# Storing the last group in chunks, counting the conditions earlier, and loading one input group in halves

## The chip, the cores and the metric

The kernel runs on one core of a Trainium2 chip. The metric is device time in microseconds (us). The engines are TensorE (PE, with PEld for its weight loads), VectorE (DVE), ScalarE (ACT), GpSimd (POOL) and SyncE (SP); SP and POOL issue the transfers here.

## What is computed

Attention with 32 inducing points, then a hardswish feed-forward block, for x of 4 x 12480 x 128:

```python
def _attn_ref(x, inducing):
    B, N, C = x.shape
    scale = 1.0 / np.sqrt(C)
    I = np.broadcast_to(inducing[None], (B, m, C))
    def mab(q, kv):
        s = scale * (q @ kv.transpose(0, 2, 1))
        s = s - s.max(-1, keepdims=True)
        a = np.exp(s)
        a /= a.sum(-1, keepdims=True) + 1e-09
        return a @ kv
    h = mab(I, x)
    return mab(x, h)

def _moe_ref(x, w_in, w_out):          # 128 -> 2048 -> 128
    h = x @ w_in
    return (h * np.clip(h + 3.0, 0.0, 6.0) / 6.0) @ w_out
```

## The kernel before

**Tiling.** Each of the 4 batches of 12480 tokens is cut into six full groups of 2048 tokens (128 partitions x 16, 1 MB of float32) and a rest of 192 (48 x 4). A group is cut into chunks of 4 tokens per partition (512 tokens), so a batch has 25 chunks and the program 100. Group g is full for 0 to 5; group 6 is the rest.

**Two phases per batch.** The first (names with `a_`, and `a_first` for batch 0) casts x to bf16 (`xb`), transposes it on PE (`pt`, copied to `xT`), forms the weights of the 32 points (`s`, then `Exp` to `a`) and sums `hnd`. From this the coefficients follow (`c_` functions, `c_first` for batch 0): the transposed summary `HT` by way of `htp` and the reciprocal `rD`, its bf16 differences `dH`, the products `gp` and `dpm`, the squares `sq`, and at the end `Cq` and `BD`. The second phase (`b_`) makes the output chunk by chunk: `b_pack` and `b_spread` give the factor tile `d` (SP copies one quarter of `dk` over the partitions, 128 KB), `b_base` gives `TF` through `bp` on PE and Exp on ACT, `b_prod` multiplies `TF` by `d` on DVE to `TD`, `b_lin` and `b_quad` accumulate `op` on PE, `b_r` gives the factor `r_all`, and `b_evac` multiplies `op` by it into `os` on DVE.

**Order.** The schedule is written out by hand: the main loop (line 873) goes through the 100 chunks, and in batch b's chunks the work of batch b + 1 is interleaved by shares. In iteration t it first evacuates chunk t - 1, then works on PE for chunk t; `TD` is made one iteration ahead. The two `op` buffers in PSUM mean that chunk t needs the evacuation of chunk t - 2. The last batch has nothing to interleave. For batch 0, `a_first` works in half groups: per piece, cast (partly on ACT, partly on DVE), transposes of the next piece, weights, sum of the piece before.

**Queues.** POOL issues all loads of x and of the weights, and the stores of batches 0 to 2; SP issues the spreads of `d` and the stores of the last batch. On each the order of the program is kept. A full group of output is one store of 1 MB after its fourth chunk (line 842).

**The end.** The second phase rests on conditions on the data (bounds on the factors, the denominators and the hidden values). After the last chunk five counts on DVE (lines 924 to 939) look over all of them, PE sums the counts over the partitions (`cp5`, line 941), DVE compares the sum with the expected number (`bad_i`), and only then `b_evac` of the last chunk follows (line 946). All engines load `bad_i` (line 949) and branch on it (line 952): a direct path is there for data that don't meet the conditions. The path isn't taken here.

**Dummy products.** `warm(n)` issues n products on a zero tile, so that PE stays busy; `c_first` has them at lines 629, 633 and 635.

Of the kernel before, what the change touches and what calls it, by code (L numbers as in the profile page):

```python
# [9 lines left out]
FP32 = mybir.dt.float32  # L10
# [4 lines left out]
ALU = mybir.AluOpType  # L15
AX = mybir.AxisListType
# [8 lines left out]
TG = 16  # L25
SL = 4
XBUF = 5
# [13 lines left out]
def kernel(  # L41
# [8 lines left out]
    nc = tc.nc  # L50
    P = nc.NUM_PARTITIONS
    B, N, C = x.shape
    M = inducing.shape[0]
# [15 lines left out]
    NGR = len(groups)  # L69
# [4 lines left out]
    NCK = len(chunks)  # L74
    first_chunk = [chunks.index((g, 0)) for g in range(NGR)]

    keep = ctx.enter_context(tc.tile_pool(name="keep", bufs=1))
# [3 lines left out]
    with ExitStack() as es:  # L81
# [14 lines left out]
        cst = es.enter_context(tc.tile_pool(name="cst", bufs=1))  # L96
# [10 lines left out]

        xs, xbs = {}, {}

        def load_x(b, g, parts=1):  # L110
            t0, p, n = groups[g]
            src = x[b, t0 : t0 + p * n, :].rearrange("(p i) c -> p i c", i=n)
            if n < TG:
                t = xlast.tile([P, n, C], FP32R, name="xl")
            elif b == 0 and g == XBUF:

                t = osp.tile([P, TG, C], FP32R, name="x5", tag="os")
            else:
                t = xin.tile([P, TG, C], FP32R, name="xr")
            for h in range(parts):  # L120
                lo, hi = h * n // parts, (h + 1) * n // parts
                nc.gpsimd.dma_start(t[:p, lo:hi, :], src[:, lo:hi, :])
            xs[(b, g)] = t

        load_x(0, 0, 2)

        held = []
        NF = NGR - 1 if rest else NGR
# [34 lines left out]

        make_identity(nc, ident[:, :])
        for g in (NF, *range(1, XBUF + 1)):
            load_x(0, g, 2 if g in (XBUF - 1, XBUF) else 1)
        wake = const.tile([P, 512], BF16, name="wake")
        nc.vector.memset(wake[:, :], 0.0)
        ident_b = const.tile([P, P], BF16, name="ident_b")
# [2 lines left out]
        def warm(n):  # L172

            wp = psF.tile([P, 512], FP32, name="wp", tag="fb")
            for _ in range(n):
                nc.tensor.matmul(wp[:, :], lhsT=wake[:, :P], rhs=wake[:, :])
# [34 lines left out]
        NR = B * NCK * SL  # L211
# [415 lines left out]
        def c_first():  # L627

            warm(2)
            nc.scalar.copy(w_in_b[:, : F // 2], w_in_r[:, : F // 2].bitcast(FP32))  # L630
            c_den(0)
            nc.scalar.copy(w_in_b[:, F // 2 :], w_in_r[:, F // 2 :].bitcast(FP32))
            warm(2)
            c_HT(0)
            warm(1)

            def cast_w(i, j):
                nc.scalar.copy(w_out_b[:, i:j, :], w_out_r[:, i:j, :].bitcast(FP32))

            cast_w(0, 4)  # L640
            c_G(0, 0, 6)
            sq = lambda *jbs: [c_sq(0, jb) for jb in jbs]
            cs = lambda *jcs: [c_C(0, jc) for jc in jcs]

            sg = lambda jb: (c_sq(0, jb), c_G(0, jb + 6, jb + 7))
            sg(0)
            sg(1)
            sg(2)
            cast_w(4, 8)
            b_pack(0, 0)  # L650
            b_e(0, 0)
            for c in range(4):
                b_spread(0, c)
            load_held(3)
            for jb in range(3, 7):
                sg(jb)
                cs(jb - 3)
            cast_w(8, 12)
            sg(7)
            b_f(0, 0)  # L660
            cs(4)
            sg(8)
            b_base(0, 0, 0)
            cs(5)
            sg(9)
            c_hs(0)
            b_base(0, 0, 1)
            cs(6)
            cast_w(12, 16)
            sq(10)  # L670
            cs(7)
            sq(11)
            b_r(0, 0)
            cs(8)
            sq(12)
            cs(9)
            sq(13)
            cs(10)
            b_base(0, 1, 0)
            sq(14)  # L680
            cs(11)
            sq(15)
            cs(12)
            c_L(0, 0)
            c_L(0, 1)
            b_base(0, 1, 1)
            a_cast(1, 0, ((nc.scalar.copy, 0, 2), (nc.scalar.copy, 2, 4)))
            b_prod(0, 0)
            c_BD(0)
            cs(13, 14, 15)  # L690
            c_tail(0)
            b_pack(0, 1)
            b_e(0, 1)
            c_max(0)
# [131 lines left out]
        def b_evac(b, c, op):  # L826
            g, j = chunks[c]
            t0, p, n = groups[g]
            st = S[b]
            if j == 0:  # L830
                st["os"] = osp.tile([P, TG, C], FP32, name="os", tag="os")
            ot = st["os"]
            nc.vector.tensor_mul(  # L833
                ot[:p, j * SL : (j + 1) * SL, :],
                op[:p, :].rearrange("p (s c) -> p s c", c=C),
                r_all[:p, b, c, :].unsqueeze(2).to_broadcast([p, SL, C]),
            )
            if (j + 1) * SL == n:
                r0 = b * N + t0

                eng = nc.gpsimd if b < B - 1 else nc.sync
                eng.dma_start(  # L842
                    out[r0 : r0 + p * n, :].rearrange("(p i) c -> p i c", i=n), ot[:p, :n, :]
                )


        a_begin(0)
        a_first()
        c_first()
        queue = []  # L850
        total = B * NCK
        ahead, sums = {}, {}
        for b in range(B):
            for g in range(NGR):
# [18 lines left out]
        for t in range(total):  # L873
# [10 lines left out]
            def bg(part):  # L884
                fill(n_units * (t - begin + part) / span)

            if t == total - NCK // 2:

                nc.gpsimd.drain()
# [29 lines left out]
            b_quad(bo, co, 3, op)  # L919
            evac = (bo, co, op)  # L920

        cnt = cst.tile([P, 5], FP32, name="cnt")
        junk = cst.tile([P, NR], FP32, name="junk", tag="r6")
        nc.vector.tensor_scalar(
            junk[:, :NR], r_all[:, :, :, :].rearrange("p b c s -> p (b c s)"), 1.0e-16, None,
            op0=ALU.is_ge, op1=ALU.add, accum_out=cnt[:, 0:1],
        )
        nc.vector.tensor_scalar(
            junk[:, : B * NGR], nf_all[:, :], -1.0e-8, None, op0=ALU.is_le, op1=ALU.add, accum_out=cnt[:, 1:2]
        )  # L930
        nc.vector.tensor_scalar(
            junk[:, :B], g_all[:, :], 3.0, None, op0=ALU.is_le, op1=ALU.add, accum_out=cnt[:, 2:3]
        )
        nc.vector.tensor_scalar(
            junk[:, : B * M], d_all[:, :, :].rearrange("p b m -> p (b m)"), 1.0e-20, None, op0=ALU.is_ge, op1=ALU.add, accum_out=cnt[:, 3:4]
        )
        nc.vector.tensor_scalar(
            junk[:, : B * M], d_all[:, :, :].rearrange("p b m -> p (b m)"), 1.0e30, None, op0=ALU.is_le, op1=ALU.add, accum_out=cnt[:, 4:5]
        )
        cp5 = psF.tile([P, 512], FP32, name="cp5", tag="fb")  # L940
        nc.tensor.matmul(cp5[:1, :5], lhsT=ones[:, 0:1], rhs=cnt[:, :])
        cs = cst.tile([1, 1], FP32, name="cs")
        nc.vector.tensor_reduce(cs[:, :], cp5[:1, :5], axis=AX.X, op=ALU.add)
        good = float(P * (NR + B * NGR + B + 2 * B * M))
        nc.vector.tensor_scalar(bad_i[:, :], cs[:, :], good, None, op0=ALU.not_equal)
        b_evac(*evac)


    bad = nc.values_load(
# [150 lines left out]
```

## Time and profile before

| | us |
|---|---|
| median of 4 runs (312.69 to 313.84) | 313.65 |
| the profiled execution, whole | 313.53 |
| its span, first to last instruction | 311.7 |
| PE busy | 299.2 |
| DVE busy | 236.5 |
| ACT busy | 231.6 |
| granted PE clock, mean | 0.993 |
| last matmul of the last chunk ends | 304.9 |
| store of the last full group issued / of the rest issued | 304.5 / 307.3 |

All times of the profile are us from the start of the span. A row of the timeline gives start, length, engine, line, operation, output<-input and shape, and in brackets the idle time before it and what ended it. A row of a tile's or line's view gives durations in ns (smallest, median, largest) and the first and last start. Instructions that only issue transfers, wait or branch are not counted as busy; they stand under the engine's queue (SPq for SP's).

### The profile page before, as it was taken

How to read it: one execution, taken by the hardware profiler on the slowest of the kernel's cores; microseconds unless marked ns; L12 is line 12 of the kernel's file. 1: busy time of each engine (PE TensorE's matmuls, PEld its weight loads, DVE VectorE, ACT ScalarE, POOL GpSimd, SP SyncE). 2: the span in 40 equal slices, each digit the busy share in tenths (PEclk: the TensorE clock that was granted, in tenths of full speed). 3: DMA queues.
4: the chain of work that ended last, by engine and by line, in shares of the span. 5: the costliest groups of instructions: out<-in, count | busy, mean ns of one | idle time of the engine just before them, and what ended most of it. 6: DMA issues, size and time to landing. Idle time of an engine off the chain costs nothing.

```text
span 311.7 us, 9605 instructions
## 1 busy us (share of the span) xinstructions
PE 299.2 (96%) x3930; PEld 233.5 (75%) x3930; DVE 236.5 (76%) x539; ACT 231.6 (74%) x425; POOL 34.6 (11%) x81
## 2 busy tenths in 40 slices
PE   8799999999999999999999999999999999999991
PEld 3697678887676878888767877888867786777781
DVE  1797796978883868878796668787788477888883
ACT  3788999886589678886679859888658945777750
POOL 7511301111100010101110000100000001000000
PEclk9999999999999999999999999999999999999997
DMA  6999496988963452899965525555255335566654
GB/s 208 413 393 349 97 381 212 313 315 249 374 210 105 133 174 67 295 302 322 331 201 188 176 70 161 174 187 183 57 170 182 146 76 191 172 209 216 212 185 156
DMA packets 24513, 66.69 MB, mean 214 GB/s; under 512 B 3104, under 2 KB 17472, under 8 KB 18576
## 3 DMA queue, kind: packets, MB, share of 16 engines
q0 software_dynamic: 9088, 46.83, 43.3%
q1 hardware_dynamic: 15376, 19.19, 22.3%
q8 instruction: 32, 0.52, 0.7%
q14 instruction: 17, 0.14, 0.1%
HBM read 27.67 MB, written 25.56 MB: 171 GB/s over the span
## 4 chain that ended last, share of the span: by engine, by line
PE 77%; ACT 11%; DVE 6%; DMA 2%; issue 2%; POOL 1%; ACTq 0%; DVEq 0%; POOLq 0%
PE op L817 26%; PE bp L777 12%; PE op L801 7%; PE hnd L290 6%; ACT sq L579 6%; PE pt L268 5%; PE cp L588 4%; PE s L276 2%; PE pp L748 2%; ACT TF L784 2%; DMA xr<-in_x_dram 2%; PE hnd L392 2%; PE pt L369 2%; PE ep L704 2%; PE dpm L568 2%
## 5 line engine op out<-in xcount | busy, mean ns | idle before, releaser
L784 ACT ACTIVATE TF<-bp 128x512 bf16<-128x512 f32 (+1 forms) x200 | 117.3, 599 | 38.6 <-PE rp L737 20.9
L817 PE MATMUL op<-Cq,TF 128*128 128x128 bf16 (+1 forms) x800 | 109.2, 223 | 0.0
L817 PE MATMUL op<-Cq,TD 128*128 128x128 bf16 (+1 forms) x800 | 105.9, 219 | 0.0
L833 DVE TENSOR_TENSOR os<-op,r_all 128x512 f32<-128x512 f32 (+1 forms) x100 | 68.4, 684 | 19.6 <-PE op L817 18.7
L817 PEld LDWEIGHTS <-TF 128*128 128x128 bf16 (+1 forms) x800 | 50.5, 98 | 33.6 <-issue 25.1
L777 PE MATMUL bp<-xT,W 128*128 128x512 bf16 (+1 forms) x200 | 75.1, 376 | 0.1
L793 DVE TENSOR_TENSOR TD<-TF,d 128x1024 bf16<-128x1024 bf16 (+1 forms) x100 | 66.8, 668 | 0.7 <-ACT TF L784 0.4
L817 PEld LDWEIGHTS <-TD 128*128 128x128 bf16 (+1 forms) x800 | 61.4, 98 | 0.6
L801 PE MATMUL op<-BD,nf 128*128 128x512 f32 (+1 forms) x100 | 53.3, 533 | 0.5 <-DVE os L833 0.3
L579 ACT ACTIVATE sq<-dpm 128x512 bf16<-128x512 f32 x60 | 35.2, 641 | 4.5 <-PE dpm L568 2.2
L259 ACT CAST xb<-xr 128x1024 bf16<-128x1024 f32 x36 | 37.6, 1055 | 0.0
L738 DVE RECIPROCAL r_all<-rp 128x4 f32<-128x4 f32 (+1 forms) x100 | 17.7, 177 | 24.3 <-PE rp L737 23.8
L737 PE MATMUL rp<-one,nf 128*128 128x4 f32 (+1 forms) x100 | 34.5, 345 | 0.4
L269 DVE COPY xT<-pt 128x1024 bf16<-128x1024 bf16 (+1 forms) x42 | 25.8, 617 | 8.3 <-PE pt L268 7.8
L842 POOL DMA_DIRECT2D out_dram<-os x21 | 11.3, 538 | 143.1 <-DVE os L833 136.4
L290 PE MATMUL hnd<-xr,a 128*32 128x128 f32 x288 | 24.1, 226 | 0.0
L755 ACT ACTIVATE dk<-pp 128x512 bf16<-128x512 f32 (+1 forms) x28 | 15.7, 560 | 10.4 <-PE pp L748 10.4
L568 PE MATMUL dpm<-dH,w_in_b 128*128 128x512 bf16 x64 | 23.3, 381 | 0.0
L268 PE MATMUL pt<-ident_b,xb 128*128 128x128 bf16 x300 | 23.3, 218 | 0.0
L777 PEld LDWEIGHTS <-W 128*128 128x128 bf16 x200 | 19.5, 97 | 5.0 <-issue 3.4
L588 PE MATMUL cp<-w_out_b,sq 128*128 128x128 bf16 x256 | 22.7, 220 | 0.5 <-ACT sq L579 0.5
L510 PE MATMUL gp<-HTr,w_in_r 128*128 128x32 f32 x64 | 21.3, 358 | 0.2 <-ACT HTr L488 0.2
(129 smaller groups left out, 407.3 us busy)
## 6 DMA issues: line engine op xcount, KB each, us to landing
xr<-in_x_dram POOLq DMA_DIRECT2D x21, 1024.0 KB, 8.3
out_dram<-os POOLq DMA_DIRECT2D x18, 1024.0 KB, 4.5
d<-dk SPq DMA_DIRECT2D x96, 128.0 KB, 3.7
out_dram<-os SPq DMA_DIRECT2D x6, 1024.0 KB, 4.1
xr<-in_x_dram POOLq DMA_DIRECT2D x4, 512.0 KB, 8.5
x<-in_x_dram POOLq DMA_DIRECT2D x2, 512.0 KB, 14.0
w_in_r<-in_moe_w_in_dram POOLq DMA_DIRECT2D x1, 1024.0 KB, 13.8
w_out_r<-in_moe_w_out_dram POOLq DMA_DIRECT2D x1, 1024.0 KB, 16.6
```

The costliest lines, as they stand in the source:

```text
L259: eng(xb[:p, lo:hi, :], xs[(b, g)][:p, lo:hi, :].bitcast(FP32))
L268: nc.tensor.transpose(pt[:, (i - lo) * p : (i - lo + 1) * p], xb[:p, i, :], ident_b[:p, :p])
L290: nc.tensor.matmul(st["hnd"][:M, :C], lhsT=a1[:p, i * M : (i + 1) * M], rhs=xs[(b, g)][:p, i, :], start=(g == 0 and i == 0), stop=(g == NG ...
L579: nc.scalar.activation(sq[:, :], dpm[:, :], ACT.Square)
L588: nc.tensor.matmul(st["cp"][:, k * C : (k + 1) * C], lhsT=sq[:, k * P : (k + 1) * P], rhs=w_out_b[:, jc, :], start=(jc == 0 and k == 0), s ...
L737: nc.tensor.matmul(rp[:p, :SL], lhsT=nf[:, j * p : (j + 1) * p], rhs=one4[:, :])
L777: nc.tensor.matmul(bp[:, :w], lhsT=st["W"][:, k].rearrange("p m i -> p (m i)"), rhs=st["xT"][:, c0 : c0 + w],)
L784: nc.scalar.activation(st[("x", c)][:, k, :w], bp[:, :w], ACT.Exp, scale=scale)
L793: nc.vector.tensor_mul(u[:, :, :w], t[:, :, :w], d[:, :w].unsqueeze(1).to_broadcast([P, 2, w]))
L801: nc.tensor.matmul(op[:p, :], lhsT=st[("nf", g)][:, j * p : (j + 1) * p], rhs=st["BD"][:, :], start=True, stop=False, skip_group_check=True,)
L817: nc.tensor.matmul(op[:p, s * C : (s + 1) * C], lhsT=T[k][:, s * p : (s + 1) * p], rhs=st["Cq"][:, k, :], start=False, stop=(s == SL - 1 a ...
L833: nc.vector.tensor_mul(ot[:p, j * SL : (j + 1) * SL, :], op[:p, :].rearrange("p (s c) -> p s c", c=C), r_all[:p, b, c, :].unsqueeze(2).to_ ...
```

## The change

It has four parts.

1. The last full group of the last batch is stored chunk by chunk: four stores of 256 KB (2 KB a partition) instead of one of 1 MB.
2. The conditions are counted in seven counts in place of five. Six are made inside the last batch, ahead of the evacuation in iterations t = 84 (two), 87, 91 and 98 (two). The seventh, over the last chunk's 4 columns of `r_all`, stands behind the loop. The evacuation of the last chunk now follows it, ahead of the sum on PE and of the verdict.
3. Group 1 of batch 0 is loaded as two transfers of 512 KB.
4. In `c_first`, `c_HT` goes ahead of the dummy products, and there are two where there were two before it and one behind it.

```diff
-        def load_x(b, g, parts=1):
+        def load_x(b, g, cuts=(0, TG)):
...
-            for h in range(parts):
-                lo, hi = h * n // parts, (h + 1) * n // parts
+            for lo, hi in zip(cuts, cuts[1:]):
+                lo, hi = min(lo, n), min(hi, n)
                 nc.gpsimd.dma_start(t[:p, lo:hi, :], src[:, lo:hi, :])
...
-            load_x(0, g, 2 if g in (XBUF - 1, XBUF) else 1)
+            load_x(0, g, (0, 8, 16) if g in (1, XBUF - 1, XBUF) else (0, TG))
...
+            c_HT(0)
             warm(2)
-            c_HT(0)
-            warm(1)
...
-            if (j + 1) * SL == n:
+
+            single = b == B - 1 and g == NF - 1
+            if single or (j + 1) * SL == n:
                 r0 = b * N + t0
+                lo, hi = (j * SL, (j + 1) * SL) if single else (0, n)
 
                 eng = nc.gpsimd if b < B - 1 else nc.sync
                 eng.dma_start(
-                    out[r0 : r0 + p * n, :].rearrange("(p i) c -> p i c", i=n), ot[:p, :n, :]
+                    out[r0 : r0 + p * n, :].rearrange("(p i) c -> p i c", i=n)[:, lo:hi, :], ot[:p, lo:hi, :]
                 )
+
+        total = B * NCK
+        NCHECK = 7
+        cnt = keep.tile([P, NCHECK], FP32, name="cnt")
+        r_rows = r_all[:, :, :, :].rearrange("p b c s -> p (b c s)")
+        checks = []
+
+        def check(values, limit, op):
+            n = values.shape[1]
+            junk = cst.tile([P, 512], FP32, name="junk", tag="r6")
+            k = len(checks)
+            nc.vector.tensor_scalar(
+                junk[:, :n], values, limit, None, op0=op, op1=ALU.add, accum_out=cnt[:, k : k + 1]
+            )
+            checks.append(n)
+
+        def early_checks(left):
+
+            r_of = lambda i, j: check(r_rows[:, i * SL : j * SL], 1.0e-16, ALU.is_ge)
+            d = d_all[:, :, :].rearrange("p b m -> p (b m)")
+            if left == 16:
+                check(g_all[:, :], 3.0, ALU.is_le)
+                check(d, 1.0e-20, ALU.is_ge)
+            elif left == 13:
+                check(d, 1.0e30, ALU.is_le)
+            elif left == 9:
+                r_of(0, (B - 1) * NCK)
+            elif left == 2:
+                check(nf_all[:, :], -1.0e-8, ALU.is_le)
+                r_of((B - 1) * NCK, total - 1)
...
+            early_checks(total - t)
             if t == total - NCK // 2:
...
-        cnt = cst.tile([P, 5], FP32, name="cnt")
-        junk = cst.tile([P, NR], FP32, name="junk", tag="r6")
...
+        check(r_rows[:, (total - 1) * SL :], 1.0e-16, ALU.is_ge)
+        b_evac(*evac)
         cp5 = psF.tile([P, 512], FP32, name="cp5", tag="fb")
-        nc.tensor.matmul(cp5[:1, :5], lhsT=ones[:, 0:1], rhs=cnt[:, :])
+        nc.tensor.matmul(cp5[:1, : len(checks)], lhsT=ones[:, 0:1], rhs=cnt[:, :])
...
         nc.vector.tensor_scalar(bad_i[:, :], cs[:, :], good, None, op0=ALU.not_equal)
-        b_evac(*evac)
```

The lines left out in the last part are the five counts of before, and the sum and comparison, which now go by the number of counts.

## The prediction

> **What bounds the kernel now.** I read the busy row first: TensorE (PE) is busy 96% of the span. A kernel in that state gains nothing from a faster vector engine; it gains where PE has no work. So the next view is the table of stages at the end of the run.
>
> ```profile
> PE 299.2 (96%) x3930; PEld 233.5 (75%) x3930; DVE 236.5 (76%) x539; ACT 231.6 (74%) x425; POOL 34.6 (11%) x81
> 290.00:300.00 10.00, 10.00 (x124) 7.99 (x124) 8.41 (x20) 7.95 (x16) 0.00 (x0) 1.00 0.60 201
> 304.00:306.00 2.00, 0.94 (x16) 0.77 (x14) 1.86 (x11) 0.00 (x0) 0.00 (x0) 1.00 0.42 160
> 308.00:312.00 4.00, 0.00 (x0) 0.00 (x0) 0.00 (x0) 0.00 (x0) 0.00 (x0) 0.50 0.14 41
> ```
>
> After the length come busy us of PE, PEld (weight load), DVE (VectorE), ACT (ScalarE), POOL, then clock, DMA share, GB/s. PE fills 290 to 300 and has finished at 304.94 (last row 304.66 + 0.28). The span ends at 311.7, so 6.7 us lie behind the last product. The timeline says who owns them:
>
> ```profile
> 303.47 0.36 DVE L793 TENSOR_TENSOR TD<-TF,d 128x384 bf16<-128x384 bf16 x1 [0.28 <-DMA d<-dk]
> ...
> 303.84 0.65 DVE L833 TENSOR_TENSOR os<-op,r_all 128x512 f32<-128x512 f32 x1
> ...
> 304.41 0.55 DVE L924 TENSOR_SCALAR_CACHE_REDUCE junk<-r_all 128x400 f32<-128x400 f32 x1
> ...
> 304.52 3.11 SPq L842 DMA_DIRECT2D out_dram<-os  x2
> ...
> 306.52 0.14 DVE L945 TENSOR_SCALAR bad_i<-cs 1x1 int32<-1x1 f32 x1
> 306.60 0.67 DVE L833 TENSOR_TENSOR os<-op,r_all 48x512 f32<-48x512 f32 x1
> ```
>
> DVE evacuates chunk 23, runs five counts and the verdict, and evacuates chunk 24 only at 306.60, though PE had it ready at 304.94. SP stores the whole last full group at 304.52 and the remainder at 307.29. Then the branch on the verdict:
>
> ```profile
> L949 DVEq TENSOR_LOAD <-bad_i x1: 1041/1041/1041, 306.7 to 306.7; - x1
> L949 SPq TENSOR_LOAD <-bad_i x1: 519/519/519, 307.7 to 307.7; - x1
> L952 SPq EVENT_SEMAPHORE  x7: 17/17/17, 308.4 to 309.5; - x7
> DMA to landing us min/median/max: 2.1/4.2/4.7
> ```
>
> SP's load of the verdict is last (307.68 to 308.20), as it is queued behind the remainder's store issue. SP then checks seven DMA semaphores at 67 to 83 ns each, except that the third comes only at 309.23: the 1 MB store issued at 304.52 lands after 4.7 us, at 309.21. That wait holds 0.71 us. From 309.23 to 311.66 is fixed closing code. (The last line is the store line's own issues from 285 on.)
>
> The start, in ACT's timeline and the chain:
>
> ```profile
> 10.70 0.62 ACT L359 CAST xb<-xr 128x512 bf16<-128x512 f32 x1 [1.09 <-DMA xr<-in_x_dram]
> ...
> 13.13 0.62 ACT L359 CAST xb<-xr 128x512 bf16<-128x512 f32 x1 [0.43 <-DMA xr<-in_x_dram]
> ```
> ```profile
> 26.13 0.43 PE wp L176 x2
> 26.56 0.19 PE htp L479
> ...
> 26.78 0.23 DVE HT L482
> ```
>
> ACT waits for x group 1 (landed 10.60) and again for group 2 (13.11). Later two dummy products stand ahead of the transpose htp on the path.
>
> **The counts and the last stores.** I rebuild the tail from 302.47, where DVE has ended the reciprocal of chunk 23. Steps are start to start of the present rows: count over nf 0.22 (305.01 to 305.23), over g 0.20, over d (128 columns) 0.33. The new count over 96 columns lies between the last two: 0.30. So 0.52 us of counts now stand ahead of the evacuation of chunk 22: 303.01 instead of 302.49, end 303.68. Chunk 24's first product needs that PSUM buffer and started at 303.51, so it slips to 303.74, and PE ends at 305.17 (+0.23). DVE's product for chunk 24 had waited to 303.47 for a DMA; it starts at 303.61 (+0.14), chunk 23's evacuation at 303.98, end 304.63, its store is issued at 304.66. The last count (4 columns, the g row, 0.20) ends at 304.86, hidden behind PE. Chunk 24's evacuation starts at 305.21 and ends at 305.88; the remainder's store is issued at 305.91 (before 307.29). The verdict's reduction is now queued behind that evacuation: 305.88 + 0.325 (the present 306.34 to 306.665) = 306.20, 0.46 earlier than now. SP's load starts at 306.30, after the 0.33 + 0.06 of the store issue. It takes 0.52 as it did alone on SP, or 0.96 to 1.04 as on the four engines that loaded together; now all five load almost together, so 306.82 to 307.34, and I take 307.1. From load end to span end was 311.66 - 308.20 = 3.46; without the 0.71 of waiting, 2.75. End 309.85: **1.8 us gained**, bounds 1.55 to 2.1.
>
> That holds if no store is waited for. The remainder's store took 2.14 from issue to landing: 308.05, checked at about 308.9. Chunk 23's 256 KB lie between that and the 1 MB's 4.7; interpolated by size from 2.14 (96 KB) to the median 4.2 (1 MB) 2.5, so 307.2, checked near 307.6. Here a rule speaks against the change. The Trainium skill, "DMA: Bandwidth & Descriptors", section Measured, says to batch to 1 MiB or more, and its Anatomy section gives 2.0 us plus bytes over 436 GB/s for each DMA: 2.6 us a chunk. Paid one after another from the first issue at 300.08, that is 310.5, 1.3 us after the present landing, and the gain falls to 0.5. The rows speak otherwise: spreads (d, 128 KB) on this queue are issued every 1.6 us or so and land after about 4, so they overlap. I take the overlap: by the rule's 2.6 for the last chunk alone 307.3, the same answer. Three more issues of 0.34 us on SP have nothing behind them: the last spread (299.22) goes ahead of the first chunk store, and only stores follow.[...]
>
> The early counts: 0.53 us ahead of the evacuation at 277.71, 0.33 at 283.42, and about 0.48 (300 columns, by 0.59 for 400 and 0.33 for 128) at 290.75. At each, DVE sits idle 0.23 to 0.27 for PE, so evacuation and the product behind it come 0.3, 0.1 and 0.2 late. The TD tile is ready about 0.9 us before PE uses it, the PSUM buffer about 0.7 (evacuation end 280.28, needed 280.99), and DVE's next idle gaps (0.19, 0.52) win the lag back. Cost nothing; if the later slack were gone, the excess of each count over its gap (0.30 + 0.06 + 0.21), 0.6 us. A gain is excluded: they are only added work.
>
> **The dummy products.** Two of 0.43 us leave the path ahead of htp and two stand behind it, where one stood. HT needs htp and the reciprocal rD (26.17 + 0.36 = 26.53). Without the dummies htp is done before that, so HT starts at 26.56 instead of 26.78: 0.22 gained, not 0.43; rD is late next. The dummies behind htp end about 26.8, before the product gp that waits for ACT's HTr (now 27.31, then 27.09). ACT's square at 28.61 follows HT by way of dH, and ACT is then solid to 36. Its cast of w_out, which landed at 27.5, ends at 28.15, under the new start of 28.39. **0.2 gained**, bounds 0 to 0.25.
>
> **Group 1 in halves.** Its first half may land near 9.3, so the cast moves to about 9.6 (ACT's Exp of 9.22 is ahead of it) from 10.70. But the cast of group 2 waits for its own whole megabyte at 13.11, and DVE's order has its half of that cast ahead of the copy xT that PE needs at 14.41. So the 1.1 us lead becomes idle time at 13.1; I count at most 0.05 of it. Against that, halves are slower to move: 4 KB packets have a median of 174 ns and 8 KB 325 to 332, so 8 KB cost 16 to 23 ns more, with 8 such packets on each engine 0.13 to 0.18 us; by landings, group 5's halves took 2.55 (18.92 to 21.47) against 2.51 for groups 2 and 3, so 0.04. Everything behind on that queue shifts alike, both weights too. I take **0.1 lost**, bounds +0.2 and -0.05. POOL pays one more issue of 0.54 us: group 5's second half, its constants and the weight issues (10.31, 10.89) move 0.4 to 0.6 later, covered by a queue that is full to 27.5. If that cover were gone, w_out would land at 28.1 and ACT's cast end at 28.75, 0.36 late.
>
> **Sum.** Span 311.7 - 1.8 - 0.2 + 0.1 = 309.8. The profiled execution took 313.53, 1.83 around its span: 311.6. It lies 0.12 below the median 313.65; so 311.7.
>
> **Rivals.**
> A, as worked out: 311.7, 310.9 to 312.4. Chance 0.69.
> B, a store takes the place of the removed wait: chunk 23's 256 KB, issued at 304.66, land as late as the 1 MB's 4.7 did, 309.36, so the old wait at 309.23 stays. For it: the present landings have one straggling engine (fifteen at 308.24 to 308.41, the last at 309.21). Against it: a quarter of the bytes. The tail then gains nothing: 313.5 (no change); landing halfway, 308.5, gives 312.6. Chance 0.12 together.
> C, group 1's lead is kept: 1.1 us more, 310.6. Only if group 2 landed earlier, which halves can't bring. Chance 0.10.
> D, slower: the PE clock. PE, fed earlier by group 1, has a hole before group 2 at 13.8, about 1 us long by the sum above. The Trainium skill, "TensorE: Matmul & The Clock Gate", Part 1, puts half clock after an idle window of about 3.4 us. If the clock fell, the 3.4 us of solid PE work behind (14 to 24 is busy 10.00 of 10) would take twice as long: 311.7 + 3.4 = 315.1. It decides from a granted clock under 1.00 in 11 to 17 us. The rows show 1.00 from 0 to 40, even where PE was busy 2.43 of 4 us. Chance 0.04, and 0.05 remains for mishaps between.
> That the change does not do what it says can be left out: the changed program's order of instructions has four chunk stores, the counts at their places, one dummy less and group 1 as two transfers.
>
> **Numbers.** About 0.3% (0.94 us) is what a measurement of this kernel can tell from no change, so faster means under 312.7. A and C lie there, and of B those that land before about 308.5: faster 0.84, same 0.11, slower 0.05. The range takes A and half of B and of C: 310.8 to 312.8.
>
> **What would show it.** The remainder's store issued near 305.8 (305.91 less the head's 0.1); no SP semaphore step over 0.1 us behind the verdict load (else B); the load ended 1 us or so earlier; HT 0.2 earlier against the last hnd product; the cast of group 1 near 9.6 but group 2's still at 13.1 to 13.3 (earlier: C); clock 1.00 throughout (else D). Wrong altogether if PE shows gaps near the early counts, or if chunk 24's d lands later than 303.5 because the chunk stores crowd it.

## The result and the profile after

The changed kernel takes 312.40 us (median of 42 runs, 311.75 to 314.35) against 313.49 for the kernel before (63 runs, 312.46 to 314.82) in the same sitting. The ratio of the runs is 0.9979, 95% interval 0.997 to 0.9988: 0.66 us less, where the prediction had 1.9. The medians differ by more, 1.09, because the runs of the changed kernel form two groups: 26 of the 42 lie at 312.92 or below, 16 at 313.14 or above. A second sitting of the same kernel gave 313.17 against 313.04, ratio 0.9992 (0.9979 to 1.0006). So by the ratio the change gains a third of what was forecast, and in one sitting nothing that can be told, though the median of 312.40 lies in the forecast range. The first profiled execution took 312.51 with a span of 310.7, 1.0 less than the span of before.

The table of stages of that execution, with the columns of before (length, PE, PEld, DVE, ACT, POOL, clock, DMA share, GB/s):

```profile
290.00:300.00 10.00, 10.00 (x127) 7.88 (x119) 8.35 (x22) 7.83 (x16) 0.00 (x0) 1.00 0.58 188
304.00:306.00 2.00, 1.45 (x21) 1.00 (x18) 1.68 (x7) 0.00 (x0) 0.00 (x0) 1.00 0.53 192
308.00:312.00 4.00, 0.00 (x0) 0.00 (x0) 0.00 (x0) 0.00 (x0) 0.00 (x0) 0.81 0.09 26
```

PE is as full from 290 to 300 as before, now with one count more on DVE inside (two records). The tail, in the timeline:

```profile
303.14 0.69 DVE L832 TENSOR_TENSOR os<-op,r_all 128x512 f32<-128x512 f32 x1
...
304.31 0.65 DVE L832 TENSOR_TENSOR os<-op,r_all 128x512 f32<-128x512 f32 x1
304.89 0.14 DVE L859 TENSOR_SCALAR_CACHE_REDUCE junk<-r_all 128x4 f32<-128x4 f32 x1
...
305.36 0.68 DVE L832 TENSOR_TENSOR os<-op,r_all 48x512 f32<-48x512 f32 x1 [0.32 <-PE op L816]
...
306.14 0.14 DVE L963 TENSOR_SCALAR bad_i<-cs 1x1 int32<-1x1 f32 x1
```

Chunk 24 is evacuated at 305.36 instead of 306.60, as soon as PE has it, and the verdict stands at 306.14. SP issues the remainder's store at 306.07, 1.22 earlier. What follows that, by line (durations in ns, first and last start):

```profile
L966 DVEq TENSOR_LOAD <-bad_i x1: 552/552/552, 306.3 to 306.3; - x1
L966 SPq TENSOR_LOAD <-bad_i x1: 522/522/522, 307.3 to 307.3; - x1
```
```profile
L969 SPq EVENT_SEMAPHORE  x7: 17/17/17, 308.0 to 308.5; - x7
...
L969 PEldq COMPARE_BRANCH  x2: 95/612/1130, 306.9 to 307.2; - x2
```

The loads of the verdict take half as long as before (552 against 1041 on DVE). But SP's issue of the remainder's store took 1202 ns here, so SP's load begins only at 307.32, and SP passes chunk 23's semaphore at 308.41. It comes there so late by its own slow issue that it hardly waits (no step is over 0.1 us), but it could not have passed earlier: fifteen of that store's sixteen parts had landed by 307.14, the last at 308.39. What most likely made that part late stands in the DMA queues of the stretch 304 to 307.5 (packets, MB, share):

```profile
q1 hardware_dynamic: 314, 0.56, 43.0%
q8 instruction: 1, 0.02, 2.4%
```

One packet of 16 KB, a load of code, started at 305.54 and took 1364 ns (the times of single packets and parts are in the trace's records; no view lists them). In the profile of before there is such a packet too, at 304.38, and the 1 MB store's late part (fifteen by 308.41, the last at 309.21) was the "straggling engine" that the prediction saw and could not name. The trace names no engine for a packet; that code and late part share one is inferred, from the comparison of all profiles below.

The start, in ACT's timeline, and the chain around HT:

```profile
9.73 0.62 ACT L359 CAST xb<-xr 128x512 bf16<-128x512 f32 x1 [0.40 <-DMA xr<-in_x_dram]
...
13.40 0.62 ACT L359 CAST xb<-xr 128x512 bf16<-128x512 f32 x1 [1.27 <-DMA xr<-in_x_dram]
```
```profile
26.59 0.37 DVE rD L473
...
27.05 0.24 DVE HT L482
```

Group 1 is cast 0.97 earlier, and the lead is idle time at group 2, 1.27 instead of 0.43, as forecast. HT follows rD at once.

### The profile page after: what moved, and what is told of

It reads as the page before. It is cut to its first block, busy times and chain, and to the rows that moved or that the text cites. A ratio compares the mean times of both kernels' runs of the same rounds, so it can differ in the third digit from the quotient of the medians.

```text
span 310.7 us, 9612 instructions
## 1 busy us (share of the span) xinstructions
PE 299.1 (96%) x3929; PEld 233.5 (75%) x3929; DVE 236.0 (76%) x543; ACT 232.0 (75%) x425; POOL 35.4 (11%) x82
## 4 chain that ended last, share of the span: by engine, by line
PE 76%; ACT 11%; DVE 5%; DMA 3%; issue 2%; POOL 1%; ACTq 0%; DVEq 0%; POOLq 0%
PE op L816 27%; PE bp L776 12%; PE op L800 7%; PE hnd L290 6%; ACT sq L579 6%; PE pt L268 5%; PE cp L588 4%; DMA xr<-in_x_dram 3%; PE s L276 2%; PE pp L747 2%; ACT TF L783 2%; PE hnd L392 2%; PE ep L703 2%; PE dpm L568 2%; PE sp L717 1%
```

## The experiments

In each, the ratio is to the kernel before, run on the same chip in the same sitting. "Tail" is the time in the profile from the start of chunk 20's evacuation to the end; it was 12.33 before (299.36 to 311.69) and 10.93 after (299.74 to 310.67).

### The parts one by one

**Without the halves** (the changed kernel):

```diff
-            load_x(0, g, (0, 8, 16) if g in (1, XBUF - 1, XBUF) else (0, TG))
+            load_x(0, g, (0, 8, 16) if g in (XBUF - 1, XBUF) else (0, TG))
```

> The changed kernel with group 1 loaded whole again; tail and dummy products stay changed. Theory H (the halves move group 2's landing back and all the program shifts by it): group 2's cast on ACT goes from 13.40 back to about 13.13, ACT's first square from 28.87 to about 28.4 to 28.6, and the time is 0.3 to 0.4 us under the changed kernel, some 1.3 to 1.5 under the one before. Rival R (the later landing is scatter of the transfers from run to run): the cast stays near 13.4 or is as late as it is early, and the time is that of the changed kernel.

Measured 311.89 (6 runs, 311.52 to 312.77), 0.995 (0.9932 to 0.9968), tail 10.56. The best ratio up to here, but from six runs; what it owes to the halves is taken up below.

**The halves alone** (the kernel before):

```diff
-            load_x(0, g, 2 if g in (XBUF - 1, XBUF) else 1)
+            load_x(0, g, 2 if g in (1, XBUF - 1, XBUF) else 1)
```

> The kernel before with group 1 in halves and nothing else. Theory H: cast of group 2 near 13.4, the time 0.25 to 0.4 us over the kernel before. Rival R: no difference beyond 0.1. A third case, the lead of group 1 is kept after all: faster by 0.3 or more.

Measured 313.70 (22 runs), 1.0005 (0.9995 to 1.0016). ACT's timeline shows where the loss that there is arises:

```profile
12.91 0.62 ACT L359 CAST xb<-xr 128x512 bf16<-128x512 f32 x1 [1.32 <-DMA xr<-in_x_dram]
...
19.35 1.05 ACT L359 CAST xb<-xr 128x1024 bf16<-128x1024 f32 x1 [0.43 <-DMA xr<-in_x_dram]
```

Group 2 is not late, but group 4's second half lands at 19.33 instead of 18.92. Its slack in the kernel before was 0.12 us (landed 18.92, cast 19.04), so 0.3 of the 0.4 reach PE: chunk 0 is evacuated at 44.23 against 43.92.

**More halves** (groups 1, 2 and 3, kernel before) and **none** (groups 4 and 5 whole too):

```diff
-            load_x(0, g, 2 if g in (XBUF - 1, XBUF) else 1)
+            load_x(0, g, 2 if g in (1, 2, 3, XBUF - 1, XBUF) else 1)
```
```diff
-            load_x(0, g, 2 if g in (XBUF - 1, XBUF) else 1)
+            load_x(0, g, 1)
```

> The kernel before with groups 1, 2 and 3 in halves, beside 4 and 5. Theory H, in proportion: group 4's second half lands 1.0 to 1.5 us later than before's 18.92, ACT's cast of it waits, and the time is 0.8 to 1.3 over the kernel before. If the price is paid once (the extra issue on POOL, or a slot of its queue), it is 0.4 as with group 1 alone. Rival R: no difference beyond 0.1, or a gain, since groups 2 and 3 are fed earlier.

> The kernel before with groups 4 and 5 of batch 0 loaded whole too, so that only group 0 is in halves. Theory H (each group in halves costs the stream 0.3 to 0.7 us): group 5 lands at 20.2 to 20.9 instead of 21.47, w_in at 23.0 to 23.6 instead of 24.11; the cast of group 4 must wait for its whole megabyte, near 18.3 instead of 18.03, so the time gains less than that or nothing, -0.3 to +0.3. Rival R (halves cost nothing, the later landings came from elsewhere): group 5 and w_in land within 0.15 of before.

Three more groups in halves: 313.59 (14 runs), 1.0017 (1.0002 to 1.0031); w_in landed at 24.99 against 24.11, chunk 0 was evacuated at 44.46. None: 315.45 (6 runs), 1.0072 (1.0051 to 1.0092). Group 5 landed at 21.39, hardly before the 21.47 of its halves, so whole transfers win nothing there; but group 4's first cast must wait for its whole megabyte:

```profile
18.91 0.62 ACT L359 CAST xb<-xr 128x512 bf16<-128x512 f32 x1 [1.29 <-DMA xr<-in_x_dram]
```

That is 1.09 of the loss (chunk 0 is evacuated at 45.01). The rest arises at the end of this execution, where PE's second branch took 3417 ns instead of 417, of which more below.

**The chunk stores alone** (kernel before):

```diff
-            if (j + 1) * SL == n:
+            single = b == B - 1 and g == NF - 1
+            if single or (j + 1) * SL == n:
                 r0 = b * N + t0
+                lo, hi = (j * SL, (j + 1) * SL) if single else (0, n)
...
-                    out[r0 : r0 + p * n, :].rearrange("(p i) c -> p i c", i=n), ot[:p, :n, :]
+                    out[r0 : r0 + p * n, :].rearrange("(p i) c -> p i c", i=n)[:, lo:hi, :], ot[:p, lo:hi, :]
```

> The kernel before with only the last full group stored chunk by chunk; all five counts and the verdict stay at the end. Theory F (chunk 23's store has one late part because an instruction fetch holds one transfer engine, and lands 2.5 to 3.4 us after its issue): the landing is before SP's semaphores at 308.4, nothing is waited for and the 0.7 us of the old wait are gained: span 0.7 shorter. With the run of the early counts alone (0.2 to 0.3 longer in its tail) this would say that the two parts pay only together. Rival: the chunk's store still ends the run, under 0.3 gained.

Measured 312.76 (22 runs, 312.35 to 313.28), 0.9983 (0.9973 to 0.9992), tail 11.71. Here the wait that the prediction named is gone and no other takes its place:

```profile
L955 SPq EVENT_SEMAPHORE  x7: 17/17/17, 308.4 to 308.8; - x7
L955 PEldq COMPARE_BRANCH  x2: 95/256/417, 307.3 to 307.6; - x2
```

SP's load began at 307.68 as before, and the span fell by 0.70, the old wait. By the ratio (0.53 us) this part alone brings nearly all that the whole change brings (0.66).

**The early counts without the chunk stores** (changed kernel):

```diff
-            single = b == B - 1 and g == NF - 1
+            single = False
```

> The changed kernel with the last full group stored as one megabyte again; the early counts stay. Theory S (SP's issue of the remainder's store took 1.20 us in place of 0.33 because it came close behind a run of chunk stores): the issue is 0.33 again, SP's load of the verdict starts near 306.5, and the closing code then waits for the megabyte, issued at 305.0 and landed 4.2 to 4.7 later, 309.2 to 309.7: the end is 311.4 to 312.0, 0.7 to 1.3 over the changed kernel. Rival I (the long issue comes from an instruction fetch that holds a transfer engine): the issue is as long as in the changed kernel.

Measured 313.97 (22 runs), 1.0014 (1.0006 to 1.0023). SP's load began 1.3 us earlier, but took 1051 ns with the megabyte in flight, and SP then stood at the 1 MB store to 309.17, as late as before (309.23): for SP, early counts alone win nothing. The end of this execution is not SP's, though. PE's second branch took 3545 ns, and PE's closing code ended 0.6 us after SP's:

```profile
L969 PEldq COMPARE_BRANCH  x2: 95/1820/3545, 307.5 to 307.8; - x2
```

**The remainder's store on ACT's queue** (changed kernel):

```diff
-                eng = nc.gpsimd if b < B - 1 else nc.sync
+                eng = nc.gpsimd if b < B - 1 else nc.scalar if b == B - 1 and g == NF else nc.sync
```

> The changed kernel with the store of the remainder of the last batch issued by ACT, idle by then, in place of SP. Theory S: SP's load of the verdict starts near 306.4 instead of 307.32 and the span ends 0.9 us earlier, unless a store is waited for. Rival W (chunk 23's last part, which landed at 308.39, binds next): SP is early but stands at that store's semaphore, and the end moves by 0.1 at most.

Measured 312.47 (22 runs), 0.9981 (0.9969 to 0.9994), tail 10.95: no gain. SP loaded at 306.06, reached chunk 23's semaphore at 307.08 and left it at 308.19, since that store's last part landed only at 308.17 (fifteen by 306.91; a packet of code had started at 305.75). So the 1202 ns issue cost nothing, and what the prediction called rival B is at work.

**The order of the dummy products alone** (kernel before):

```diff
-            warm(2)
             c_HT(0)
-            warm(1)
+            warm(2)
```

> The kernel before with only the order of the dummy products changed. Both theories: HT starts 0.1 to 0.2 us earlier after the copy of H than before (1.46 us), as in the three runs so far that have it (1.31 to 1.33); the first square 0.15 earlier after H (3.14 against 3.29). Theory: this stays to the end, 0.15 us under the kernel before. Rival: w_out's landing (27.4 to 27.5) catches the square and less than 0.1 is left.

Measured 313.84 (20 runs, 313.37 to 315.05), 1.0024 (1.0013 to 1.0034): slower, though HT came 1.32 after the copy of H instead of 1.46. The lost time is at the end, and on PE:

```profile
L951 PEldq COMPARE_BRANCH  x2: 95/1794/3492, 307.6 to 307.9; - x2
```

PE's second branch took 3492 ns, against 417 before, and PE's closing code ended 1.5 us after SP's (311.51 and 309.98). This execution had no code packet near 304; one came at 309.02, 1.13 after the branch had begun. And the 1 MB store, issued at 304.30, landed whole at 308.20, without a late part: SP waited for nothing. So the wait of 0.71 in the kernel before seems to come from the code packet beside the store, not from the store's size. The Trainium skill, "Runtime: NRT & Kernel Launch", section Instruction fetch mechanics, has the mechanism: code comes in 16 KiB blocks of 256 instructions, ahead of time and in sequence, and a taken branch to a block that is not there has to wait for it. The trace agrees in the block (32 packets of 16 KB for PE's 7898 records, one per 250 or so; a record is one instruction in the trace) and gives the price here, 3.1 us.

### Is it the last load of code?

Two theories stood from here. P: one dummy product less is two PE instructions less, so the last block boundary moves towards the very end of PE's program, and its load comes late or not at all. Q: a load of code and a store race, whatever the count.

**Chunk stores and order together** (the two edits above, kernel before):

> The kernel before with the chunk stores and with HT ahead of the dummy products; counts and halves as before. Alone, the chunk stores gave 0.9983 of before and the order gave 1.0024, although HT came 0.15 us earlier against H in its profile; its time was lost at the end, where PE's closing branch took 3492 ns instead of 417, because the code that it jumps to had not been loaded ahead. Theory Q (the load of that code, one 16 KB packet due near 304 us, is kept out by the 1 MB store that is issued within 0.2 us of it; chunk stores leave room for it): the two edits add up without that loss, PE's branch takes 0.4 to 1.2 us, the time is 0.15 under that of the chunk stores alone, 0.998 of before, about 312.6. Theory P (PE's program is two instructions shorter, and that moves the code's blocks so that the target is not loaded ahead): the branch takes 3.4 to 3.5 us here too and PE's end comes last; since PE's branch starts near 307.4, the end is 311.8, about 313.5 to 313.8 whole, 1.001 to 1.002 of before.

Measured 312.89 (22 runs, 312.28 to 314.78), 0.9996 (0.9984 to 1.0009), and a branch of 3250 ns in the profile. Q's claim that chunk stores leave the load its room falls with that branch; P's time (1.001 to 1.002) was not met either, so the branch is hardly late in every execution.

**The order with all three dummies kept** (kernel before):

```diff
-            warm(2)
             c_HT(0)
-            warm(1)
+            warm(3)
```

> The kernel before with HT ahead of all three dummy products, none taken out, so PE has as many instructions as before. Theory P (two PE instructions fewer displace the code's blocks): nothing is displaced here, PE's closing branch takes 0.42 us and the gain of 0.15 at HT is kept: 0.9995 of before or 313.1 to 313.2. Theory Q (a race between the load of the code and the 1 MB store, which falls either way): the branch takes 0.4 in some executions and 3.5 in others, the times have two humps 1.2 us or so apart as those of before have, and the ratio lies between 0.9995 and 1.0025. If the ratio is near 1.0025 again, the order, not the count, is what costs.

Measured 312.97 (22 runs), 1.0001 (0.9991 to 1.0011), branch 417 ns, HT 1.31 after H. Against 1.0024 with a dummy less, the intervals are just apart: the order costs nothing that can be told, the missing dummy some 0.7 us.

**Without the halves, the store on ACT**, as a candidate for the best version (both edits above):

> The changed kernel without the halves of group 1, and with the remainder's store issued by ACT instead of SP. Without the halves alone 0.995 of before. With the store moved alone, SP loaded the verdict 1.2 us earlier and then stood at the semaphore of chunk 23's store. Theory 1 (that store's late sixteenth part sets the end): the two edits together give what the first gives, 0.995 (311.9 in that run); the wait at that semaphore only gets longer, 0.7 to 1.2 us. Rival: SP's way to the verdict sets the end in most executions, and the store of chunk 23 only where its packets stand behind a load of code; then up to 0.3 us more, 0.994 or 311.6.

Measured 312.49 (14 runs), 0.9978 (0.9963 to 0.9993), tail 10.91, with SP at chunk 23's semaphore from 307.40 to 308.48. Not better than the change, and the expected 0.995 of the six runs without halves is not borne out. This execution lost time at the start in another way: the granted clock fell (columns as above).

```profile
11.00:12.00 1.00, 0.99 (x11) 0.80 (x12) 0.16 (x2) 1.00 (x2) 1.00 (x1) 0.57 1.09 418
12.00:13.00 1.00, 1.00 (x12) 0.94 (x11) 0.94 (x2) 0.70 (x3) 0.13 (x1) 0.50 1.05 418
```

**The changed kernel once more**, unedited:

> The changed kernel unchanged, for a second profile and more executions in one sitting with the three others. Its times so far have two humps, 311.8 to 312.9 and 313.1 to 314.4. Theory Q in the form that the upper hump is an execution whose code was not loaded ahead: if the profiled execution is of the upper hump, PE's closing branch takes about 3.5 us; if it is of the lower, about 1.1. Rival: the upper hump comes from the start, and the profile of an upper execution then has its first square and first evacuation a microsecond or so later (28.9 and 44.2 so far), with the same end. Median expected 312.4, 0.997 to 0.999 of before.

Measured 313.17 (22 runs, 311.75 to 314.60), 0.9992 (0.9979 to 1.0006), where a median of 312.4 was expected. Its profile is the key to the case. Up to chunk 24's evacuation (305.32) it is the first one within 0.1 us; then:

```profile
L969 SPq EVENT_SEMAPHORE  x7: 17/17/17, 307.1 to 307.5; - x7
...
L969 PEldq COMPARE_BRANCH  x2: 95/1736/3377, 306.9 to 307.3; - x2
```

No code packet lies between 296.24 and 307.92. Chunk 23's store is whole at 307.17, SP's issue of the remainder's store took 331 ns, behind the same chunk stores, so the 1202 of the first execution is not their doing. SP waits for nothing and is through at 307.61, 1.96 before its time in the kernel before: the gain of the prediction. And it buys nothing, because PE's branch runs from 307.33 to 310.71 and the span ends at 311.65, tail 11.95. So the same code either loads the block in time, and its packet delays the store, or doesn't, and PE waits. Neither P nor Q alone says which; it differs between executions.

The tie holds in all twenty profiles. In ten the branch took over 0.5 us, and in each it ended 1.19 to 1.44 us after the end of a code packet: in six the packet started 0.6 to 1.2 us after the branch (3.25 to 3.57 us), in four it had ended 0.3 to 0.4 us ahead of it (0.76 to 1.14). In the other ten it had ended at least 1.6 us ahead, and the branch took 0.33 to 0.43. The last store ahead of the remainder's tells the other half: in the six profiles with a late branch its sixteenth part came 0.00 to 0.01 us after the fifteenth (0.27 in one), and in the nine others of unshifted code 0.29 to 1.26.

### Moving the load of code

The direct test of the cause moves the block boundaries. Dummy products at the start are made narrower, so that the same columns take more PE instructions:

```diff
-        warm(8)
+        warm(5)
+        warm(24, 64)
```

(`warm(n, m)` uses m columns.) That is 42 more PE records. On the changed kernel and on the kernel before:

> The changed kernel with three of its eight 512-column dummy products at the start replaced by 24 of 64 columns: the same columns, 42 more records of PE. PE goes through about 25 records per us at the end, so its load of code comes about 1.7 us earlier, near 303.5 to 304, ahead of chunk 23's store (issued 304.94) and well ahead of the branch. Theory P (the place of that load holds back the gain): no upper hump, the branch takes 0.42 us, SP doesn't wait at a store's semaphore, SP's chain ends as in the second profile of the changed kernel at 307.6, and the span is 307.61 + 2.12 = 309.7, 311.5 to 311.7 whole, 0.994 to 0.996 of before. Rival (the load's place is chance, or something else makes the humps): two humps as for the changed kernel and 0.997 to 0.999.

> The kernel before with the same three dummy products replaced, 42 more records of PE. Its load of code, at 304.38 in the profile and 0.14 us ahead of the 1 MB store, comes near 302.7. Theory P: the store has no late sixteenth part (fifteen parts had landed by 308.41, the last by 309.21), so up to 0.7 us of the wait at its semaphore goes; the branch always takes 0.42 and the upper hump goes: 312.2 to 312.7, 0.997 to 0.999 of the kernel before. Against the same shift of the changed kernel this leaves 0.9 to 1.2 us of real gain of the tail. Rival: 1.000 with both humps.

Both became slower, 1.0028 (1.0019 to 1.0038) and 1.0039 (1.0028 to 1.005), against the expectation. But the tails are as the theory has them: branches of 425 and 328 ns, no step over 0.1 us at SP's semaphores, 11.90 before and 10.33 after, 1.58 between them. The loss lies elsewhere, here in the kernel before so shifted (DVE's timeline, then code and store in the queues of 258 to 266, with the us from issue to landing; last the same store in the kernel before unshifted):

```profile
264.81 0.69 DVE L834 TENSOR_TENSOR os<-op,r_all 128x512 f32<-128x512 f32 x1 [2.04 <-DMA out_dram<-os]
```
```profile
q8 instruction: 1, 0.02, 1.4%
...
out_dram<-os POOLq DMA_DIRECT2D x1, 1024.0 KB, 6.2
...
out_dram<-os POOLq DMA_DIRECT2D x1, 1024.0 KB, 4.2
```

Another block's load, at 259.6 where it had been at 263.4, now falls on a 1 MB store of batch 2. The store lands after 6.2 us instead of 4.2, its buffer is free 2.0 us late, and the evacuation, then PE, stand. The changed kernel so shifted has the same stall, 1.87, and its profile lost further time at the start (chunk 0's evacuation at 45.22), where the granted clock was 0.50 from 8.9 to 12.3.

**The same without halves, and the other direction** (the changed kernel without its four dummy products around HT, 8 fewer PE records):

```diff
-            warm(2)
...
             c_HT(0)
-            warm(2)
```

> The changed kernel without the halves of group 1 and with the 42 more PE records. If the halves cost the 0.3 us that the landings of the weights showed (24.6 against 24.1 for w_in), this is 0.3 us under the shifted changed kernel. If they cost nothing (in two profiles the first evacuation came at 44.24 without and 44.19 with them), the two are equal within 0.1. If they help, because PE is busier ahead of group 2 and its clock doesn't fall (in one profile without halves it was granted 0.50 from 11.4 to 14.6), this one is slower by up to 0.3, by way of executions with a mean clock of 0.991 or less.

> The changed kernel without the four dummy products around HT, 8 fewer PE records. The other direction: the load of code is due about 0.3 us later than in the changed kernel, when PE has almost nothing left. Theory P: it is missed in nearly all executions, PE's branch takes 3.3 to 3.5 us, and nearly all times lie in the upper hump, 313.1 to 314.4, median 313.6, 1.001 to 1.002 of before. Rival (chance): humps shared as in the changed kernel, median 312.4 to 313.2.

Without halves 313.09 (14 runs), 0.9999 (0.9986 to 1.0013): the same stall, here 1.38 us, and the tail 10.32. This is 0.9 us under the same kernel with halves, of which the stall accounts for 0.5 in the profiles; the rest isn't explained. With fewer instructions 313.63 (22 runs), 1.0019 (1.0004 to 1.0035): branch 3572 ns, tail 11.99, as P had it. But the time is only in part P's: 15 of the 22 runs have a mean granted clock of 0.991 or less, so without these dummies the clock fell as well. The seven others took 312.07 to 313.52, six of them 313.1 or more.

**Twice as far**, to get the load at 259.6 ahead of that store:

```diff
-        warm(8)
+        warm(2)
+        warm(48, 64)
```

> The changed kernel with six of the eight dummy products at the start replaced by 48 of 64 columns: 84 more records of PE, about 3.4 us at the end's 25 records per us. Load theory: the load that lay at 263.4 in the kernel before and at 259.6 with 42 more records comes near 257.5, ahead of the 1 MB store issued at 258.5; that store lands in about 4.2 us again and the stall of 2.0 us goes; the last load comes near 302; the tail stays at 10.3 us. Then the span is 309.7 to 310.1, the time 311.5 to 311.9, 0.994 to 0.996 of before, unless one of the other thirty loads now falls on another store. Rival: the stall is not tied to the load's place but to the narrow dummies at the start; then 1.003 as with 42.

> As the run beside it, without the halves of group 1. With 42 more records the kernel without halves was 0.3 per cent faster than the one with them (0.9999 against 1.0028 of before), but there the stall in the middle differed too (1.38 against 1.87 us). If the halves cost what the landings of the weights show, this is 0.3 to 0.5 us under its neighbour; if they cost nothing, equal.

With halves 311.91 (6 runs, 311.73 to 311.98), **0.9952** (0.9938 to 0.9967). Without, 311.78 (6 runs, 311.67 to 312.02), 0.9948 (0.9934 to 0.9963). The first one's rows:

```profile
L970 SPq EVENT_SEMAPHORE  x7: 17/17/17, 307.5 to 307.9; - x7
L970 PEldq COMPARE_BRANCH  x2: 95/254/414, 307.3 to 307.6; - x2
```
```profile
263.82 0.69 DVE L833 TENSOR_TENSOR os<-op,r_all 128x512 f32<-128x512 f32 x1
```
```profile
out_dram<-os POOLq DMA_DIRECT2D x1, 1024.0 KB, 4.3
```

The branch is short, SP waits for no store, the store of batch 2 lands in 4.3 and the stall is gone. The last load of code comes at 303.50; the late parts are now those of the stores of chunks 20 and 21 (whole at 306.06 and 306.55, 1.2 and 1.0 after their fifteenth parts), and nobody waits for them. Tail 10.06, and twelve runs within 0.35 us. These have the lowest ratios seen, beside the 0.995 of the six runs without halves. The kernel before with 84 more records was not run, so how much of the 0.9952 is the shift's own gain is not shown.

## Why the prediction was wrong

**The tail: 1.8.** The rebuilt times held: remainder's issue at 306.07 and 306.03 against 305.91 less the head's 0.1, verdict done at 306.28 and 306.24 against 306.20, counts ahead of the evacuation hidden (chunk 20 follows chunk 5 by 27.07 us before and after), loads of the verdict 0.47 to 0.55 rather than 0.96 to 1.04. Chunk 24's `d` landed at 303.85, past the 303.5 that was to be a sign of error, but against chunk 20's evacuation only 0.09 later than before (4.11 and 4.02). For SP alone the sum was right: through at 307.61 in the second profile, 1.96 earlier.

The step that failed is "From load end to span end was 311.66 - 308.20 = 3.46; without the 0.71 of waiting, 2.75". It takes SP as the last engine, its wait as gone and all else as fixed. In one execution chunk 23's store could not be passed before 308.39 in place of the old wait (that SP's issue had been slow made no difference, as the run with ACT's queue showed). In the other PE's branch became the end. In the kernel before it looks harmless:

```profile
L952 PEldq COMPARE_BRANCH  x2: 95/256/417, 307.8 to 308.1; - x2
```

PE is through with it at 308.52, and with its closing code 2.24 us ahead of SP. But the branch's length is not fixed: where its code wasn't there it took 3.0 us more, which is more than that lead. So of 1.8 the first profile shows 1.40, and the profiles with a late branch (tail 13.20 with the order alone, 11.95 and 11.99 after) show 1.2 between them. Ahead of the tail 0.38 was lost (0.26 by the first evacuation), which leaves the 1.0 of the span. Where the load of code is out of the way, the tail gains 1.58 and, twice as far, more (10.06 against 11.90, though at different shifts).

The rule weighed there, to batch to 1 MiB, was rightly set aside: the four stores overlapped and landed 2.2 to 4.1 us after issue in the two profiles of the changed kernel (chunk 23's 3.40 and 2.23, where the prediction had 2.5), and cutting the store was worth 0.70 of span by itself. The sum on it was wrong: a landing at 310.5 would have set the end 1.3 later than before, not left a gain of 0.5, since the wait at the store takes the place of SP's path. Rival B had the right place (chunk 23's semaphore) and the right sign (one late engine), but weighed it by the bytes; what goes with the late part is a packet that has nothing to do with the size.

**The dummy products: 0.2.** The sum at HT was nearly right: 1.31 to 1.32 from H to HT instead of 1.46, so 0.15. The step failed in what it left out. It counted the dummy taken away as PE time and not as two instructions in the stream. With the same order, three dummies gave 1.0001 and two gave 1.0024. That is 0.7 us against 0.15, so this part of the change loses on the kernel before; on the changed kernel it was not tested by itself. It is also the likeliest reason why the ratio shows 0.66 where the profiles differ by 1.0: executions with a late branch seem more frequent after than before. In profiles of kernels with PE's count of before, one of six has it; with two or more instructions fewer, five of nine. The sample is too small to call that shown.

**The halves: 0.1 lost.** The mechanism held (lead lost at group 2, all behind later). The term was too small: what stands behind on the queue landed 0.4 to 0.5 later (`w_in` at 24.51 with the halves alone, 24.61 in the changed kernel, 24.11 before), where the prediction had 0.04 to 0.18. Chunk 0's evacuation came 0.3 later with the halves alone, as the slack at group 4's second half was 0.12 and not looked at. With the changed order it came at 43.99 to 44.19 in four profiles with halves and at 43.55 and 43.70 in two without. What a whole run loses stays open: kernels that differ in the halves alone are 0.0005 apart (the kernel before), 0.003 apart (the changed kernel, and again with 42 more records), 0.0003 (with the store on ACT's queue) and 0.0004 (84 more).

**Counts at nothing, rival C:** as argued; PE has no gaps there, and no lead was kept. **Rival D**, the clock, was taken as a thing of the halves, at 3.4 us. It fell to 0.50 for 3.41 us at the start in three of twenty profiles: from 11.1 in one without halves (above), from 9.7 with the chunk stores and the order, from 8.9 in a shifted one with halves. The first two reach chunk 0's evacuation 0.7 and 0.35 later than a profile with the same start and no such dip (3.41 us at half clock can't lose more than 1.7). The Trainium skill, "TensorE: Matmul & The Clock Gate", Part 1, has a free-running window of 3.4 us; the dips agree with its length, but PE was busy 1.96, 1.83 and 1.53 us of the 3.4 ahead of them, so no whole idle window stands there in the rows. In the profiles without such a dip the mean clock is 0.992 or more. Of the runs whose clock is on record, 38 of 248 of the kernel before lie at 0.991 or less, on average 0.7 us slower than the rest; of the changed kernel's, 2 of 66. So the dip seems rarer with the halves, the opposite of what rival D feared; no run tests that alone.

What stays open: why the last block is loaded ahead in some executions and not in others of the same code, and how large that share is for each kernel. Shown is that with the boundary 84 records earlier, neither loss occurs in the two profiles and the times of six runs each don't spread.

## What to carry to other kernels

When one engine's end is pulled in by a microsecond or two, look at when every other engine is through with the closing code, and add up for each: the gain is capped by the second, and by what can still make that one longer. A kernel of thousands of instructions on one engine loads its code while it runs, and here these loads and the stores got in each other's way; so adding or taking away a few instructions anywhere moves thirty packets against every store; an edit of that size has to be timed with its neighbours in count before its own merit is believed. Where a DMA lands fifteen parts together and one late, look for the packet of another queue at that time.

## What had not been expected of the hardware

- A load of code is one packet of 16 KB that takes 0.88 to 1.9 us. Stores beside it at the end landed their sixteenth part up to 1.5 us after the fifteenth, and a 1 MB store in the middle took 5.5 to 6.2 us instead of 4.2.
- PE's branch took 3.25 to 3.57 us where its code had not been loaded, 0.76 to 1.14 where the load had ended 0.3 to 0.4 us before, and 0.33 to 0.43 otherwise. On ACT, POOL, DVE and SP it took 0.04 to 0.06 throughout.
- Loading the verdict took 0.47 to 0.55 us on the engines that did it together with small stores in flight, and 0.94 to 1.15 with a 1 MB store in flight (SP's, a microsecond later, 0.52).
- An issue of the same 96 KB store on SP took 0.33 us in eight of nine profiles of kernels with this order and 1.20 in one.
